# Attention of the second batch in five steps per slice, its rows in SBUF for the mixing, sums of two batches on VectorE, and one further place per tile afterwards

## The chip, the cores and the metric

One core of one Trainium2 chip runs the whole program in one launch. The metric is device time in microseconds (us). Before the change it is 1882.68 us, the median of three runs (1882.22 to 1883.0).

## What is computed

Three stages follow each other, on 8 batches of 576 tokens with 512 channels (8 heads of 64): attention with pooled keys and values, a mixing layer with two large matrix products, and a spectral layer with two more.

```python
k_p = k.reshape(B, H, Sp, pool, D).mean(axis=3)          # Sp = 72
v_p = v.reshape(B, H, Sp, pool, D).mean(axis=3)
scores = scale * np.matmul(q, k_p.transpose(0, 1, 3, 2))
attn = np.exp(scores - np.max(scores, axis=-1, keepdims=True))
attn = attn / (np.sum(attn, axis=-1, keepdims=True) + 1e-09)
x = np.matmul(attn, v_p)                                  # -> (B, S, 512)
u = x + (x.transpose(0, 2, 1) @ U @ V).transpose(0, 2, 1) # mixing, rank 32
x1 = u + np.maximum(u @ w_ch1, 0.0) @ w_ch2
u2 = x1 + np.real(np.fft.fft(np.fft.fft(x1, axis=1), axis=2))
out = u2 + np.maximum(norm(u2) @ w_ch1b, 0.0) @ w_ch2b
```

## The kernel before

Each float32 operand of a large product is split into a high and a low part (`split`, L109 and L110: ScalarE rounds the high part, the low part is a subtraction, L104), and three products of the parts are added.

**The large products of the first layer.** The tokens are cut into blocks of 256, and two blocks make a group. Group 0 to group 5 are worked off in a loop of 16 *slices* each (`for f in range(NF)`). A slice is `st1` (12 matmuls of 512 columns into bank h0, from the transposed tokens `utx` and the weights) and `st2` of the slice before (12 matmuls into four banks, from `hh` and `hl`). `utx` has three places for blocks, so a group's two blocks need `utx` filled before its first `st1`. After group 5 come the remaining tokens and the second layer, with another product scheme.

**What runs between them.** Generators called lanes are stepped at fixed points of a slice: lane "a" (attention) at three points, "w" (weights), "p" (`pair_prep`: load the next group's rows of `ud` in transposing pieces, `load_blocks` L801, transpose them on VectorE, L832, and split them into `utx`), "prep" (loads and pooling of keys and values), later "d" (spectral layer). In lane "a" one tile of 128 rows of a batch goes through: `kq` (8 matmuls into banks s0 and s1, maxima on VectorE, L548, eight exponentials on ScalarE, L551, each with its sum read out by `accum_out`), two steps later `exp_turn` (5 transposes, copies to `e`), one step later `av` (10 matmuls into s0, the rows `x` scaled by VectorE, L571, split into `xh` and `xl`, and stored to HBM, `xd`), and two steps later the next `kq`, with `hu_mm` of the tile before behind it (two matmuls `hu<-xh`, `hu<-xl`). After five tiles `mix_split` makes `hst` from `hu`, and `mix_one` computes u of each tile: load `x` back from `xd` (`mix_load`, L595, two buffers), one matmul `hst` by `vst` into bank s1, an add on VectorE (L107), a store to `ud` (L131).

Batch 0 goes through `tile_steps` ahead of all slices. Batch 1 goes through lane "a" inside group 0, and its mixing has steps of its own behind its attention. The mixing of batches 2 to 6 stands beside the next batch's attention. Group 1 consists of tokens 512 to 1023, so it needs the first four tiles of batch 1 mixed and stored.

**What sets the order.** Up to the end of group 0 a scheduler orders the instructions of every engine from the dependencies. From group 1 on TensorE, ScalarE and VectorE keep the order in which the code emits them. All loads and stores named here are issued by SyncE's one queue (SP), in order.

Of the kernel before, what the change touches and what calls it, by code (L numbers as in the profile page):

```python
# [8 lines left out]
F32 = mybir.dt.float32  # L9
# [39 lines left out]
def kernel(  # L49
# [80 lines left out]
    def store(o, i):  # L130
        later(lambda: nc.sync.dma_start(out=o, in_=i))  # L131
# [200 lines left out]
    class Attn:  # L332
# [113 lines left out]

        def xtile(self, b):
            return self.p.tile([128, DM], F32, tag="xr", name="x", bufs=2)

# [11 lines left out]
        def tile_steps(self, b, t, alt=0, before=None):  # L461
# [21 lines left out]
            for i in range(2):  # L483
                h = slice(4 * i, 4 * i + 4)
                v = sc[i][:n, 0:288].rearrange("p (h k) -> p h k", h=4)
                nc.vector.tensor_reduce(out=mx[:n, h], in_=v, op=ALU.max, axis=AX.X, negate=True)
                for k in range(4):
                    a = 4 * i + k
                    nc.scalar.activation(out=s[:n, a], in_=v[:, k], func=ACTF.Exp, bias=mx[:n, a:a + 1], accum_out=sm[:n, a:a + 1])
            yield  # L490
# [45 lines left out]
        def kq(self, b, t):  # L536
# [9 lines left out]
            for i in range(2):  # L546
                v = sc[i][:, 0:288].rearrange("p (h k) -> p h k", h=4)
                nc.vector.tensor_reduce(out=mx[:, 4 * i:4 * i + 4], in_=v, op=ALU.max, axis=AX.X, negate=True)  # L548
                for k in range(4):
                    a = 4 * i + k  # L550
                    nc.scalar.activation(out=s[:, a], in_=v[:, k], func=ACTF.Exp, bias=mx[:, a:a + 1], accum_out=sm[:, a:a + 1])  # L551
            self.cur = sm
# [12 lines left out]
        def av(self, b, t):  # L565
# [9 lines left out]
            split(xh, xl, xf)  # L575
            store(xd[b][t], xf[:TT[t][1]])
            self.done[t] = xh, xl
# [7 lines left out]
        def mix_mm(self, b, t, x):  # L585
            r0, n = TT[t]
            o = mbank()
            mm(o, self.vst[:, r0:r0 + 128], self.hst, True, True)
# [491 lines left out]
    def lane_a(at):  # L1080
        for b in range(1, B):
            while b not in ready:
                yield
# [7 lines left out]
            for t in range(5):  # L1091
# [3 lines left out]
                yield  # L1095
                yield
                at.exp_turn()
                yield
# [5 lines left out]
                yield  # L1104
                yield
            at.hu_mm(b, 4, *at.done.pop(4))
            at.mix_split(b)
            yield
            if b in (1, B - 1):
                at.mix_load(b, 0)  # L1110
# [114 lines left out]
    for gi, js in enumerate(groups):  # L1225
# [4 lines left out]
        for f in range(NF):  # L1230
# [31 lines left out]
            for i in range(3):  # L1262
                step("a")
                if i != 1:
                    step("d")
                if prev and i < 2:
# [216 lines left out]
```

## Time and profile before

| | us |
|---|---|
| median of 3 runs | 1882.68 |
| the profiled execution's own time | 1883.03 |
| its span in the trace | 1881.3 |
| TensorE busy in the span | 1811.7 (96%) |
| VectorE, ScalarE, GpSimd busy | 1017.3, 707.2, 194.7 |
| TensorE busy between 176 and 203 us | 9.46 of 27.0 |

Times in the trace count from the span's start; 1.7 us of the run lie outside the span. Group 0's first `st1` starts at 65.61 us, group 1's at 202.87 us. The program is one long sequence of matmuls with two stretches in which TensorE stands: up to 65 us, and from 176 to 203 us.

### The profile page before, as it was taken

To read this page: it belongs to the slowest core of one execution; us is meant where nothing else is said; L and a number is where in the kernel's file an instruction comes from. 1 tells how busy PE (TensorE), PEld (TensorE's weight loads), DVE (VectorE), ACT (ScalarE), POOL (GpSimd) and SP (SyncE) were. 2 spreads that over 40 slices of the span, in tenths; PEclk is the share of its full clock that TensorE was granted. 3 is DMA by queue.
4 is the path that set the end of the run, shared out by engine and by line. 5 is a ranking of instruction groups with operands and counts; after the bars stand their busy time and mean duration, and the time that the engine had idled before them with its cause. 6 is when DMAs were issued, how large, how long until landed. Compare 5 with 4: busy or idle time off the path is not lost.

```text
span 1881.3 us, 29486 instructions
## 1 busy us (share of the span) xinstructions
PE 1811.7 (96%) x10424; PEld 1584.6 (84%) x10424; DVE 1017.3 (54%) x2265; ACT 707.2 (38%) x2072; POOL 194.7 (10%) x341
## 2 busy tenths in 40 slices
PE   5798899999999999999999999999999999999999
PEld 4676688878788788898998889899999999999998
DVE  6763566757656534444555765555554444444322
ACT  7762354555454222233333433333323323232321
POOL 3430132222200000000000000000000000000000
PEclk8899799999999999999999999999999999999999
DMA  9753547877766722567767876777677675767674
GB/s 357 265 164 103 163 159 217 247 244 256 239 197 201 206 76 73 195 221 234 229 226 264 274 223 216 242 225 232 208 229 223 191 238 173 238 180 231 183 208 134
DMA packets 265779, 394.26 MB, mean 210 GB/s; under 512 B 61664, under 2 KB 92480, under 8 KB 265632
## 3 DMA queue, kind: packets, MB, share of 16 engines
q1 hardware_dynamic: 264704, 388.97, 66.5%
q0 software_dynamic: 928, 3.40, 0.6%
q8 instruction: 83, 1.36, 0.3%
q14 instruction: 64, 0.52, 0.1%
HBM read 312.73 MB, written 79.56 MB: 209 GB/s over the span
## 4 chain that ended last, share of the span: by engine, by line
PE 68%; DVE 2%; ACT 1%; DMA 1%; issue 0%; ACTq 0%; SPq 0%; DVEq 0%
PE h L114 31%; PE o L114 16%; PE m L114 8%; PE hu L114 7%; PE s L114 4%; PE s L927 1%; DMA wr<-wc 0%; DMA wd<-cv 0%; DMA x<-x 0%; DVE hl L1307 0%; DVE side L107 0%; ACT hh L1301 0%; PE s L557 0%; ACT s L551 0%; DVE hl L1015 0%
## 5 line engine op out<-in xcount | busy, mean ns | idle before, releaser
L114 PEld LDWEIGHTS h<-x,wr 128*128 128x128 f32 x4032 | 527.7, 191 | 26.1 <-DVE side L107 2.1
L114 PE MATMUL h<-x,wr 128*128 128x256 f32 x4032 | 547.6, 284 | 1.0 <-DVE side L107 1.0
L114 PE MATMUL o<-w,hh 128*128 128x512 f32 x1152 | 328.8, 396 | 3.2 <-ACT hh L1014 3.2
L114 PE MATMUL h<-utx,w 128*128 128x512 f32 (+1 forms) x1164 | 285.8, 395 | 1.4 <-ACT utx L110 1.2
L114 PEld LDWEIGHTS h<-utx,w 128*128 128x128 f32 x1164 | 218.8, 191 | 48.4 <-DVE hl L1015 1.4
L114 PEld LDWEIGHTS o<-w,hh 128*128 128x128 f32 x1152 | 202.7, 190 | 34.4 <-ACT hh L1014 4.1
L114 PE MATMUL o<-w,hl 128*128 128x512 f32 x576 | 192.3, 392 | 0.0
L107 DVE TENSOR_TENSOR side<-h,side 128x256 f32<-128x256 f32 x192 | 106.3, 553 | 150.2 <-PE h L114 149.6
L114 PE MATMUL m<-w,hh 128*128 128x512 f32 x576 | 164.4, 394 | 0.0
L1015 DVE SCALAR_TENSOR_TENSOR hl<-h,hh 128x512 fp32r<-128x512 f32 x96 | 66.3, 690 | 153.1 <-ACT hh L1014 152.9
L1301 ACT ACTIVATE hh<-side 128x256 fp32r<-128x256 f32 x192 | 99.9, 520 | 119.4 <-DVE side L107 115.4
L1301 ACT ACTIVATE hh<-h 128x256 fp32r<-128x256 f32 x96 | 36.8, 383 | 264.5 <-PE h L114 262.3
L1307 DVE SCALAR_TENSOR_TENSOR hl<-h,hh 128x256 fp32r<-128x256 f32 x96 | 40.7, 424 | 169.5 <-ACT hh L1301 169.5
L114 PEld LDWEIGHTS o<-w,hl 128*128 128x128 f32 x576 | 108.3, 188 | 24.2
L1307 DVE SCALAR_TENSOR_TENSOR hl<-side,hh 128x256 fp32r<-128x256 f32 x192 | 105.9, 551 | 29.4 <-ACT hh L1301 28.6
L114 PEld LDWEIGHTS m<-w,hh 128*128 128x128 f32 x576 | 102.2, 189 | 16.5
L1014 ACT ACTIVATE hh<-h 128x512 fp32r<-128x512 f32 x96 | 57.1, 594 | 148.6 <-PE h L114 148.5
L114 PE MATMUL hu<-w,hh 128*128 128x512 f32 x384 | 104.8, 394 | 0.0
L551 ACT ACTIVATE s<-s,mx 128x72 f32<-128x72 f32 x280 | 85.6, 329 | 44.8 <-DVE mx L548 44.4
L114 PE MATMUL m<-w,hl 128*128 128x512 f32 x288 | 97.3, 392 | 0.0
L104 POOL TENSOR_TENSOR wo<-wo 128x256 fp32r<-128x256 f32 x88 | 67.8, 789 | 267.9 <-ACT wo L110 154.5
L104 DVE TENSOR_TENSOR x<-ul,x 128x256 fp32r<-128x256 f32 x154 | 59.3, 421 | 47.6 <-ACT x L110 47.6
(250 smaller groups left out, 2421.7 us busy)
## 6 DMA issues: line engine op xcount, KB each, us to landing
wr<-wc SPq DMA_DIRECT2D x336, 512.0 KB
wc<-wo SPq DMA_DIRECT2D x88, 256.0 KB
x<-x SPq DMA_DIRECT2D x56, 256.0 KB
ur<-ud SPq DMA_DIRECT2D x36, 256.0 KB
x1d<-ur SPq DMA_DIRECT2D x36, 256.0 KB
ul<-u2d SPq DMA_DIRECT2D x36, 256.0 KB
ur<-u2d SPq DMA_DIRECT2D x36, 256.0 KB
out<-ur SPq DMA_DIRECT2D x36, 256.0 KB
```

The costliest lines, as they stand in the source:

```text
L104: eng.tensor_tensor(out=o, in0=a, in1=b, op=ALU.subtract)
L107: eng.tensor_tensor(out=o, in0=a, in1=b, op=ALU.add)
L114: nc.tensor.matmul(o, a, b, start=start, stop=stop, skip_group_check=True)
L551: nc.scalar.activation(out=s[:, a], in_=v[:, k], func=ACTF.Exp, bias=mx[:, a:a + 1], accum_out=sm[:, a:a + 1])
L927: nc.tensor.transpose(o[:, k * 128:k * 128 + 128], u[:, k * 128:k * 128 + 128], ident)
L1014: nc.scalar.activation(out=hh, in_=o, func=ACTF.Relu)
L1015: nc.vector.scalar_tensor_tensor(out=hl, in0=o, scalar=0.0, in1=hh.bitcast(F32), op0=ALU.max, op1=ALU.subtract)
L1301: nc.scalar.activation(out=hh[:, i], in_=c, func=ACTF.Relu)
L1307: nc.vector.scalar_tensor_tensor(out=hl[:, i], in0=c, scalar=0.0, in1=hh[:, i].bitcast(F32), op0=ALU.max, op1=ALU.subtract)
```

## The change

Five edits:

1. **Steps.** In group 0 lane "a" is stepped five times per slice and not three.
2. **Rows kept.** For batch 1 `xtile` hands out a tile of the pool `wo` (five buffers, 128 x 512 values, used otherwise by the weight lanes). `av` no longer stores it; it is put into `self.xm[t]`, and lane "a" mixes tile by tile from there, one step each, with no `mix_load`. Its `mix_mm` alternates between banks s1 and s0.
3. **Sums.** In batches 0 and 1 the exponentials have no `accum_out`; one `tensor_reduce` over 8 x 72 values per partition on VectorE makes a tile's sums (10 tiles in all).
4. **Places.** From batch 2 on there is one more step between `kq` and `exp_turn` and one less between `av` and the next `kq`.
5. **Start.** Batch 2 waits until slice 15 of group 0 has come.

```diff
         def xtile(self, b):
+            if b == 1:
+                return self.wo().rearrange("p h x -> p (h x)").bitcast(F32)
             return self.p.tile([128, DM], F32, tag="xr", name="x", bufs=2)
...
-                    nc.scalar.activation(out=s[:n, a], in_=v[:, k], func=ACTF.Exp, bias=mx[:n, a:a + 1], accum_out=sm[:n, a:a + 1])
+                    nc.scalar.activation(out=s[:n, a], in_=v[:, k], func=ACTF.Exp, bias=mx[:n, a:a + 1])
+            nc.vector.tensor_reduce(out=sm, in_=s, op=ALU.add, axis=AX.X)
...
-                    nc.scalar.activation(out=s[:, a], in_=v[:, k], func=ACTF.Exp, bias=mx[:, a:a + 1], accum_out=sm[:, a:a + 1])
+                    kw = {} if b == 1 else {"accum_out": sm[:, a:a + 1]}
+                    nc.scalar.activation(out=s[:, a], in_=v[:, k], func=ACTF.Exp, bias=mx[:, a:a + 1], **kw)
+            if b == 1:
+                nc.vector.tensor_reduce(out=sm, in_=s, op=ALU.add, axis=AX.X)
...
-            store(xd[b][t], xf[:TT[t][1]])
+            if b == 1:
+                self.xm[t] = xf
+            else:
+                store(xd[b][t], xf[:TT[t][1]])
...
-            o = mbank()
+            o = bank("s0") if b == 1 and t % 2 else mbank()
             mm(o, self.vst[:, r0:r0 + 128], self.hst, True, True)
...
-            while b not in ready:
+            while b not in ready or (b == 2 and state["slot"] < NF - 1):
                 yield
...
                 yield
                 yield
+                if b > 1:
+                    yield
                 at.exp_turn()
                 yield
                 at.av(b, t)
...
                 yield
-                yield
+                if b == 1:
+                    yield
             at.hu_mm(b, 4, *at.done.pop(4))
             at.mix_split(b)
             yield
-            if b in (1, B - 1):
+            if b == 1:
+                for t in range(5):
+                    at.mix_one(b, t)
+                    yield
+            if b == B - 1:
...
                 if i != 1:
+                    if gi == 0:
+                        step("a")
                     step("d")
```

**Place 1, between group 0 and group 1.** TensorE, from the first mixing matmul of batch 1 (`hst` by `vst`) to group 1's first `st1` (`h0<-utx`). The rows with `k`, `ident` and `v` are batch 2's first tile. Before:

```order
L114 MATMUL s1_1394<-hst_1358,vst_132 128x512
L114 MATMUL s1_1420<-hst_1358,vst_132 128x512
L114 MATMUL s1_1464<-hst_1358,vst_132 128x512
L114 MATMUL s1_1510<-hst_1358,vst_132 128x512
L114 MATMUL s1_1532<-hst_1358,vst_132 128x512
L114 MATMUL s1_1579<-k_126,q_1163 128x144 x2
L557 MATMUL s0_1651<-ident_69,s_128 128x128 x2
L558 MATMUL s1_1652<-ident_69,s_128 128x128
L114 MATMUL s0_1672<-v_127,e_1658 128x128
L114 MATMUL s0_1672<-v_127,e_1658 128x192 x3
L114 MATMUL s0_1672<-v_127,e_1658 128x64
L114 MATMUL h0_1703<-utx_122,w_420 128x512 x12
```

and now:

```order
L114 MATMUL s1_1262<-hst_1259,vst_132 128x512
L114 MATMUL s0_1283<-hst_1259,vst_132 128x512
L114 MATMUL s1_1286<-hst_1259,vst_132 128x512
L114 MATMUL s0_1295<-hst_1259,vst_132 128x512
L114 MATMUL s1_1304<-hst_1259,vst_132 128x512
L114 MATMUL s0_1611<-k_126,q_1111 128x144 x2
L114 MATMUL s1_1612<-k_126,q_1111 128x144 x2
L563 MATMUL s0_1652<-ident_69,s_128 128x128 x4
L564 MATMUL s1_1653<-ident_69,s_128 128x128
L114 MATMUL h0_1672<-utx_122,w_425 128x512 x12
L114 MATMUL s0_1689<-v_127,e_1659 128x128
```

The mixing alternates banks, all of batch 2's first `kq` stands behind it (half of it and two transposes stood ahead of it before), and batch 2's first `av` has moved behind the `st1`. In both programs the mixing stands behind the 16th `st1` of group 0.

At the same place SyncE's queue, from the first store of batch 1's mixed rows (`ud`) on; `x1_` are batch 1's rows in HBM, `ul<-ud` the transposing loads. Before:

```order
L131 DMA ud_116<-x_1367 128x512
L131 DMA ud_116<-x_1369 128x512
L595 DMA x_1409<-x1_2_83 128x512
L801 DMA ul_1456<-ud_116 32x16x32 x2
L595 DMA x_1448<-x1_3_84 128x512
L801 DMA ul_1456<-ud_116 32x16x32 x2
L131 DMA ud_116<-x_1409 128x512
L131 DMA ud_116<-x_1448 128x512
L801 DMA ul_1478<-ud_116 32x16x32 x4
L595 DMA x_1486<-x1_4_85 64x512
L801 DMA ul_1567<-ud_116 32x16x32 x3
L131 DMA ud_116<-x_1486 64x512
```

and now:

```order
L131 DMA ud_116<-wo_858 128x512
L131 DMA ud_116<-wo_1001 128x512
L131 DMA ud_116<-wo_1087 128x512
L131 DMA ud_116<-wo_1163 128x512
L810 DMA ul_1334<-ud_116 32x16x32
L131 DMA ud_116<-wo_1239 64x512
L810 DMA ul_1334<-ud_116 32x16x32 x3
L444 DMA q_1617<-qT 128x4x128
L810 DMA ul_1347<-ud_116 32x16x32 x4
L810 DMA ul_1387<-ud_116 32x16x32 x4
L810 DMA ul_1417<-ud_116 32x16x32 x4
```

The three loads of `x` are gone, the stores stand together, and the sixteen transposing loads follow with one store and one load of `q` between them.

**Place 2, group 0's first product.** TensorE, from the last transposes of batch 0's rows on. Before:

```order
L817 MATMUL h0_559<-ident_69,scr14_135 128x128 x4
L817 MATMUL s1_566<-ident_69,scr15_136 128x128 x4
L114 MATMUL s0_768<-k_126,q_362 128x144 x2
L114 MATMUL h0_573<-utx_122,w_420 128x256 x24
L114 MATMUL s1_769<-k_126,q_362 128x144 x2
L557 MATMUL s0_859<-ident_69,s_128 128x128 x2
L114 MATMUL o0_706<-w_423,hh_598 128x512 x2
```

and now:

```order
L826 MATMUL h0_564<-ident_69,scr14_135 128x128 x4
L826 MATMUL s1_571<-ident_69,scr15_136 128x128 x4
L114 MATMUL h0_578<-utx_122,w_425 128x256 x24
L114 MATMUL s0_773<-k_126,q_365 128x144 x2
L114 MATMUL s1_774<-k_126,q_365 128x144 x2
L114 MATMUL o0_711<-w_428,hh_603 128x512 x2
```

Batch 1's first `kq` (`s0<-k,q`) has moved from ahead of the first `st1` to behind it.

**Place 3, a tile of batch 2 in group 1.** TensorE, from `av` (the end of it) to the next tile's `hu`. Before:

```order
L114 MATMUL s0_2061<-v_127,e_2048 128x64
L114 MATMUL h1_1836<-w_528,hh_1965 128x512 x2
L114 MATMUL h1_1836<-w_528,hl_1966 128x512
L114 MATMUL m_1840<-w_528,hh_1965 128x512 x2
L114 MATMUL m_1840<-w_528,hl_1966 128x512
L114 MATMUL h0_2092<-utx_122,w_647 128x512 x12
L114 MATMUL s0_2109<-k_126,q_1852 128x144 x2
L114 MATMUL s1_2110<-k_126,q_1852 128x144 x2
L114 MATMUL hu_1740<-xh_2069,ust_130 128x512
L114 MATMUL hu_1740<-xl_2070,ust_130 128x512
```

and now:

```order
L114 MATMUL s0_1961<-v_127,e_1946 128x64
L114 MATMUL h1_1811<-w_493,hh_1863 128x512 x2
L114 MATMUL h1_1811<-w_493,hl_1864 128x512
L114 MATMUL m_1815<-w_493,hh_1863 128x512 x2
L114 MATMUL m_1815<-w_493,hl_1864 128x512
L114 MATMUL s0_1983<-k_126,q_1719 128x144 x2
L114 MATMUL s1_1984<-k_126,q_1719 128x144 x2
L114 MATMUL hu_1733<-xh_1969,ust_130 128x512
L114 MATMUL hu_1733<-xl_1970,ust_130 128x512
```

Six matmuls stand between `av` and the next `kq`, where 18 stood; twelve matmuls of `st1` have moved from there to between `kq` and `exp_turn`.

## Rows read from the trace of the kernel before

**Rows 1.** Page, first part: busy us, share of the span, instructions.

```profile
PE 1811.7 (96%) x10424; PEld 1584.6 (84%) x10424; DVE 1017.3 (54%) x2265; ACT 707.2 (38%) x2072; POOL 194.7 (10%) x341
```

**Rows 2.** Stretches: length, busy by engine (instructions), granted clock, DMA share, GB/s.

```profile
65.60:176.00 110.40, 105.87 (x511) 87.66 (x510) 62.98 (x103) 59.11 (x169) 31.64 (x28) 0.99 0.48 150
...
176.00:203.00 27.00, 9.46 (x25) 5.88 (x25) 10.64 (x19) 5.86 (x22) 0.00 (x0) 0.58 0.60 152
```

**Rows 3.** TensorE's timeline, 50 to 100 us: start, us, instructions, [idle before].

```profile
64.66 1.33 PE L114 MATMUL s<-k,q 128*128 128x144 f32 x4 [5.89 <-ACT k L423]
65.61 3.97 PE L114 MATMUL h<-utx,w 128*128 128x256 f32 x24
...
71.12 1.20 PE L114 MATMUL o<-w,hh 128*128 128x512 f32 x4 [0.83 <-ACT hh L1014]
```

**Rows 4.** VectorE's timeline, 40 to 105 us.

```profile
51.60 1.78 DVE L153 SCALAR_TENSOR_TENSOR cv<-wraw,cv 128x512 int32<-128x512 int32 x1
53.41 0.69 DVE L104 TENSOR_TENSOR hst<-hu,hst 32x512 fp32r<-32x512 f32 x1
...
62.95 0.73 DVE L413 TENSOR_REDUCE kp<-raw 128x72 f32<-128x576 f32 x1
...
64.81 0.67 DVE L104 TENSOR_TENSOR utx<-s,utx 128x512 fp32r<-128x512 f32 x1
```

**Rows 5.** ScalarE's timeline, 0 to 42 us: the first exponentials of batch 0.

```profile
15.81 0.19 ACT L489 ACTIVATION_READ_ACCUMULATOR s<-s,mx 128x1 f32 x1
15.90 0.31 ACT L489 ACTIVATE s<-s,mx 128x72 f32<-128x72 f32 x1
```

**Rows 6.** ScalarE's timeline, 40 to 105 us: batch 1's scaled keys.

```profile
63.71 0.89 ACT L423 ACTIVATE k<-kp 64x288 f32<-64x288 f32 x2 [0.63 <-DVE kp L413]
```

**Rows 7.** TensorE's timeline, 150 to 240 us.

```profile
175.57 0.40 PE L114 MATMUL hu<-xl,ust 128*128 128x512 f32 x1
...
177.97 0.51 PE L114 MATMUL s<-hst,vst 128*128 128x512 f32 x1 [0.77 <-DVE hst L104]
...
202.87 5.30 PE L114 MATMUL h<-utx,w 128*128 128x512 f32 x12 [1.17 <-ACT utx L110]
...
215.60 1.53 PE L114 MATMUL s<-v,e 128*128 128x128 f32 x10
216.94 0.71 PE L114 MATMUL o<-w,hh 128*128 128x512 f32 x2
```

**Rows 8.** VectorE's timeline, 160 to 212 us.

```profile
178.51 0.69 DVE L107 TENSOR_TENSOR x<-s,x 128x512 f32<-128x512 f32 x1 [0.60 <-PE s L114]
...
201.44 0.71 DVE L832 STREAM_TRANSPOSE ul<-ul 128x512 f32<-128x512 f32 x1 [1.66 <-DMA ul<-ud]
```

**Rows 9.** SyncE's queue, 140 to 212 us: issues (start, us).

```profile
179.23 1.60 SPq L131 DMA_DIRECT2D ud<-x  x2
...
181.62 1.34 SPq L801 DMA_DIRECT2D ul<-ud  x2
...
196.10 2.60 SPq L801 DMA_DIRECT2D ul<-ud  x4
```

**Rows 10.** Instruction groups between 176 and 203 us: the mixing's adds.

```profile
L107 DVE TENSOR_TENSOR x<-s,x 128x512 f32<-128x512 f32 (+1 forms) x5 | 3.4, 690 | 6.8 <-DMA x<-x 5.7 <-PE s L114 1.2
```

**Rows 11.** TensorE's waits between 400 and 500 us.

```profile
PE s L557 <- ACT s L551: 1.9, 5, 1.0
```

**Rows 12.** TensorE's timeline, 305 to 345 us: two times `av`.

```profile
308.97 1.53 PE L114 MATMUL s<-v,e 128*128 128x128 f32 x10
...
322.38 1.53 PE L114 MATMUL s<-v,e 128*128 128x128 f32 x10
```

**Rows 13.** VectorE's timeline, 305 to 345 us: the scaling behind these two.

```profile
310.54 0.69 DVE L571 TENSOR_TENSOR x<-s,sm 128x512 f32<-128x512 f32 x1 [0.81 <-PE s L114]
311.99 0.69 DVE L104 TENSOR_TENSOR xl<-x,xh 128x512 fp32r<-128x512 f32 x1 [0.76 <-ACT xh L110]
...
325.56 0.68 DVE L571 TENSOR_TENSOR x<-s,sm 128x512 f32<-128x512 f32 x1
```

## What the change will do to the time

> **What bounds the kernel now.** I read first the page's busy shares: TensorE is busy 96% of the span, the next engine 54% [rows 1]. So the end moves by what TensorE waits and by what it runs at the lower clock. Then the table of stretches: between 65.6 and 176 us, which is group 0, TensorE idles 110.4 - 105.87 = 4.5 us at its full clock (0.99). Between 176 and 203 us it is busy for 9.46 of 27 us, at a granted clock of 0.58, that is mostly at its lower level of 1.2 GHz [rows 2]. The third view is TensorE's timeline at both borders. At the first product it stood 5.89 us until batch 1's scaled keys `k` came from ScalarE, because a `kq` of batch 1 stands ahead of the first `st1` in its order [rows 3]. At the second border the last matmul of batch 1's attention (`hu<-xl`) starts at 175.57, the first mixing matmul at 177.97, and group 1's first `st1` only at 202.87 [rows 7]. What lies between is one chain: mixing, store to `ud`, transposing loads, transposes, split, `st1`. SyncE's queue and VectorE's timeline tell its pace [rows 8, 9], and the groups of this stretch say that VectorE's five adds waited 5.7 us for loads of `x` [rows 10].
>
> **Border between group 0 and 1 (the main term).** The five steps per slice alone do nothing here: in the new order batch 1's last `hu` and its mixing still stand behind the 16th `st1`, as before. What changes is the chain. Half a `kq` and four exponentials of batch 2 no longer stand ahead of `hst`, so I put the first mixing matmul 1.0 us earlier, at 177.0 on the old clock face. Its add starts 0.54 us later and takes 0.69 (177.97 to 178.51, [rows 7, 8]), so it ends at 178.2, and with two banks and no loads the other adds follow at VectorE's pace. The first store is issued at 178.2. In the trace the first transposing load went out 2.4 us behind the first store, with another load between them [rows 9]; I take 2.2 us and get 180.4. Now sixteen transposing loads stand nearly together. Four in a row take 2.60 us [rows 9], so sixteen 10.4 us; with one store and one load of `q` between them (0.4 us each, an estimate below the 0.65 of a transposing load) the last is issued at 180.4 + 11.2 - 0.65 = 191.0. The last load of the old chain was issued near 198.1 (196.10 and three of four) and its transpose began at 201.44, 3.3 us later [rows 8, 9]. So the new last transpose begins at 194.3, and `st1` follows as before by 1.43 us (201.44 to 202.87), at 195.7: 7.2 us earlier. Against it: batch 2's first `av` ran inside the hole and now stands behind the `st1`. Its ten matmuls take 1.34 us from start to start (215.60 to 216.94, [rows 7]). The term is -7.2 + 1.3 = **-5.9 us**. Its ends are -3 (the loads land later when they come in one row, or batch 2's exponentials, now ahead of all four splits in ScalarE's queue, hold them up) and -8 (a last landing one microsecond faster and no `q` in the way). The hole stays some 20 us long, so I give the clock no gain: the `st1` behind it takes 5.30 us at the lower level [rows 7], before and after.
>
> The Trainium skill's page "DMA: Bandwidth & Descriptors" (section "Anatomy of one DMA — SWDGE (gpsimd) path") gives one DMA about 2.0 us fixed plus its bytes over 436 GB/s; by that a store and a load of 256 KB in a row are 2.6 us each, and the two rounds that two buffers of `x` force would be an estimated 10.4 us. The row says that VectorE lost 5.7 us to those loads [rows 10]. With 10.4 in place of the 7.2 the total would be near 1871 us. The figure is for another queue's path, and the trace decides.
>
> **Group 0's first product.** Its operands come from batch 0's `hst`, at 53.41 on VectorE; the last split into `utx` starts at 64.81 [rows 4]. In the old order 18 VectorE instructions stand from `hst` up to that split, 11.40 us or 0.63 each; 17 stand there now, 10.8 us. Ahead of `hst` there are five new sums. The nearest row is a `tensor_reduce` over 576 values per partition, 0.73 us [rows 4]: +3.7 us on VectorE. Three weight instructions of 0.7 to 1.8 us (one at 51.60, [rows 4]) have moved behind `hst`, about -3. ScalarE is relieved of 40 read-outs at 0.09 us (15.81 to 15.90, [rows 5]), 3.6 us, and VectorE waited for ScalarE there at times. I take `hst` 1 us earlier, 52.4, and the last split starts at 63.2. The first `st1` no longer waits for `k`. But its `hh` stands behind `k` on ScalarE, and `k` waits for four more VectorE instructions behind the last split, 2.8 us: 63.2 + 0.7 + 2.8 = 66.7; `k` takes 0.9 [rows 6]; I allow 0.8 for `hh` (from the end of `st1` at 69.58 to `st2` it was 1.54 with half a `kq`, [rows 3]). So `st2` starts near 68.4 and not at 71.12 [rows 3], -2.7. Since the place of `hst` is the least certain thing here I take **-2.5 us**, with ends 0 (`hst` 2 us late under the sums) and -5 (2 us earlier still).
>
> **Inside group 0.** Five more sums on VectorE, 3.7 us in 110 us of which it is busy 62.98; 3.6 us off ScalarE, busy 59.11 [rows 2]. The 4.5 us that TensorE idles there are several short waits: **0**, between -2 and +2. The stores of five tiles fall away; TensorE's order holds nothing that waits for them.
>
> **From group 1 on.** The exponentials have three steps until `exp_turn` and not two. The waits for them (1.9 us in five between 400 and 500 us, [rows 11]) can go: about -2. In return six matmuls stand between `av` and the next `kq` where 18 stood: 1.33 us, by 5.30 for twelve at half the clock [rows 7]. `kq` writes the bank that the scaling reads. The `av` of 308.97 ends at 310.50; its scaling ends at 311.23, 0.73 us behind it, and `xl` at 312.68, 2.18 behind it [rows 12, 13]. `kq` now comes at 1.33 and, with its eight matmuls at some 1.0 us, `hu<-xl` near 2.5. It fits, with 0.3 to 0.6 us to spare. For the `av` of 322.38, which ends at 323.91, scaling ended at 326.24, 2.33 us behind the end, since VectorE was busy with other work [rows 12, 13]; there `kq` would wait 1 us. Two of 28 tiles were like this in the old order; I charge +2. Batch 2 starts a slice later and so does what follows; the transposes for group 2 stand closer to their loads, and I see no wait over 2 us there. **0 us**, between -3 and +6.
>
> **Sum.** -5.9 - 2.5 + 0 + 0 = -8.4 on the profiled execution's 1883.03 us (span 1881.3 and 1.7 around it): 1874.6. That execution is 0.35 above the median of 1882.68, so **1874.3 us**.
>
> **Rivals.**
> - *The later place bites (slower).* If VectorE's scaling ends 0.6 us or more too late behind most `av`s, `kq` waits each time. Two thirds of the 30 tiles of batches 2 to 7 have the short gap: 20 x 0.6 = 12 us give 1886, 20 x 1.0 give 1894. It decides from where scaling ends over 1.33 us behind `av`. The 0.73 of the one tile speaks against it, the 2.33 of the other for it [rows 12, 13].
> - *The start gives nothing.* The sums push `hst` back by 2 us: 1874.3 + 2.5 = 1876.8.
> - *The sixteen loads hold each other up.* In one row they land 3 us later: 1877.3. The DMA share of 0.60 in the old hole leaves room [rows 2].
> - *Both, or a few microseconds late after `av`:* 1879 to 1882.
> - *The change does more than I read.* The round of store and load costs 10 us, 1871; or, against the order of TensorE, batch 1's mixing leaves the hole altogether and most of its 17.5 idle microseconds go, 1862.
>
> **How the numbers follow.** Forecast (1871.5 to 1876.5) 0.50; start gives nothing 0.15; loads hold each other up 0.11; both or a little late after `av` 0.11; more than I read 0.08; the later place bites 0.05. A measurement of this kernel tells about 0.2%, 3.8 us, from no change, so faster is below 1878.9: 0.50 + 0.15 + 0.11 + 0.08 = 0.84. The fourth is no change, 0.11, the last slower, 0.05. The range is 1868.5 to 1880.5: the ends of the two main terms give 1869.7 (-8 and -5) and 1879.7 (-3 and 0), with about a microsecond for group 0 and what follows; it leaves out the slow rival, the 1862 and the tail of the fourth case.
>
> **What would show it.** The hole: group 1's `st1` starts 19 to 21 us behind the last `hu`, with no load of `x` in it, sixteen transposing loads in one row, and a granted clock still halved. The start: no `kq` ahead of the first `st1`, `st2` near 68. After 210 us the waits of L557 for the exponentials are gone and small ones for the scaling or `xl` have come. Wrong would be: a first product later than 65.6, a hole over 25 us, or more than 5 us of waits for the scaling after 210 us.

## The result: 1892.5 us, slower by 10

The changed kernel takes 1892.47 us, the median of four runs (1891.17 to 1893.72). The kernel before took 1882.45 beside it (1880.35 to 1883.0). The ratio is 1.0055, with a 95% interval of 1.0038 to 1.0073. The forecast was 1874.3, faster; the time lies outside its range. The profiled execution took 1891.17 us, with this page (busy time, share of the span and number of instructions of an engine):

```profile
span 1889.1 us, 29426 instructions
PE 1812.9 (96%) x10424; PEld 1588.1 (84%) x10424; DVE 1029.2 (54%) x2275; ACT 700.1 (37%) x1992; POOL 191.2 (10%) x341
```

TensorE has the same 10424 matmuls and nearly the same busy time (1811.7 before). The span grew by 7.9 us through what it waits for. Where, is read by setting the same matmul of both traces side by side:

| the same matmul | before, us | after, us | difference |
|---|---|---|---|
| first `st1` of group 0 | 65.61 | 61.41 | -4.2 |
| `st1` of slice 1 | 73.07 | 70.58 | -2.5 |
| `st1` of slice 15, the last of group 0 | 171.19 | 169.69 | -1.5 |
| first `st1` of group 1 | 202.87 | 194.97 | -7.9 |
| `st1` of slice 32 | 328.08 | 321.15 | -6.9 |
| `st1` of slice 48 | 454.09 | 449.80 | -4.3 |
| `st1` of slice 69 | 617.49 | 621.16 | +3.7 |
| second layer, matmul 1008 of `h<-x,wr` | 1062.15 | 1061.95 | -0.2 |
| the same, matmul 1176 | 1113.87 | 1121.25 | +7.4 |
| the same, matmul 3948 | 1850.76 | 1858.55 | +7.8 |

One trace tells such a place to 1 or 2 us: b_spec_later below, whose code up to there is that of the kernel before, starts the `st1` of slice 15 at 169.83. So the start and the border did what was forecast, and were 7.9 us ahead at 195 us. Behind that, 11.6 us were lost between 195 and 621 us, and 4.1 more up to the end. The last rows of the table hold work that only comes later, too: the spectral lane stands a slice later, which makes the second layer's start look early (-0.2) and the next stretch look long.

**The border**, as in [rows 2, 7 to 9]. TensorE idles 13.6 us in the hole and not 17.5, still at a granted clock of 0.57. Two stretches (length, then busy time and count of PE, PEld, DVE, ACT and POOL, granted clock, DMA share, GB/s):

```profile
61.40:169.69 108.29, 102.69 (x491) 86.20 (x492) 69.66 (x107) 57.35 (x129) 35.43 (x30) 0.97 0.43 135
175.00:195.00 20.00, 6.43 (x19) 3.70 (x19) 9.82 (x18) 5.82 (x22) 0.00 (x0) 0.57 0.67 162
```

The timelines of TensorE, SyncE's queue and VectorE there (start, time taken, engine, line, instruction, count, in brackets the idle time before it and what ended it):

```profile
175.35 0.73 PE L114 MATMUL s<-hst,vst 128*128 128x512 f32 x2 [1.41 <-DVE hst L104]
194.97 4.66 PE L114 MATMUL h<-utx,w 128*128 128x512 f32 x12 [11.31 <-ACT utx L110]
```

```profile
176.61 2.20 SPq L131 DMA_DIRECT2D ud<-wo  x4
178.91 0.66 SPq L810 DMA_DIRECT2D ul<-ud  x1
183.03 8.03 SPq L810 DMA_DIRECT2D ul<-ud  x12
```

```profile
193.54 0.71 DVE L841 STREAM_TRANSPOSE ul<-ul 128x512 f32<-128x512 f32 x1 [1.22 <-DMA ul<-ud]
```

Four stores stand in one row, the first transposing load follows the first store by 2.3 us (forecast 2.2), the sixteen loads have only a store and a load of `q` between them, and `st1` follows the last transpose by 1.43 us.

**Behind the border.** What TensorE waited for between 205 and 625 us (total, times, longest), first before, then after, the two largest of each:

```profile
PE s L114 <- ACT e L560: 2.9, 4, 1.6
PE s L557 <- ACT s L551: 2.4, 7, 1.0
```

```profile
PE s L114 <- DVE x L107: 12.1, 15, 1.3
PE s L114 <- DVE x L577: 2.1, 3, 1.6
```

All such waits in this stretch add up to 6.3 us before and 17.6 us after, which accounts for 11.3 of the 11.6 us lost.

The waits for the turn of the exponentials (L557, now L563) are gone. In their place stand 15 waits for `x` of L107, 12.1 us. L107 is an addition: that of the mixing (`mix_mm`), and not the scaling (L577). One place of the fifteen, batch 3's last-but-one tile, on TensorE, VectorE and ScalarE:

```profile
306.66 1.53 PE L114 MATMUL s<-v,e 128*128 128x128 f32 x10
307.99 0.48 PE L114 MATMUL s<-hst,vst 128*128 128x512 f32 x1
309.70 0.65 PE L114 MATMUL s<-k,q 128*128 128x144 f32 x4
311.02 0.76 PE L114 MATMUL s<-k,q 128*128 128x144 f32 x4 [0.67 <-DVE x L107]
```

```profile
308.22 0.69 DVE L577 TENSOR_TENSOR x<-s,sm 128x512 f32<-128x512 f32 x1
309.67 0.69 DVE L104 TENSOR_TENSOR xl<-x,xh 128x512 fp32r<-128x512 f32 x1 [0.76 <-ACT xh L110]
310.28 0.68 DVE L107 TENSOR_TENSOR x<-s,x 128x512 f32<-128x512 f32 x1
```

```profile
309.01 0.63 ACT L110 ACTIVATE xh<-x 128x512 fp32r<-128x512 f32 x1 [1.56 <-DVE x L577]
```

The mixing matmul follows `av` on TensorE and writes bank s1. Its add stands on VectorE behind the scaling and `xl`, and `xl` waits 0.76 us for ScalarE's `xh`. So the add ends at 310.96, 2.78 us behind the end of `av` (308.18). The next tile's `kq` came 1.51 us behind that end. Its first half writes s0, which the scaling left at 308.91, and starts at once. Its second half writes s1 and waits until the add has read it. Before, `kq` came 4.24 us behind such an `av` (that of 308.97 in [rows 12]) and met a free bank; that `kq`, and the add that had left the bank at 313.28:

```profile
314.74 1.14 PE L114 MATMUL s<-k,q 128*128 128x144 f32 x8
```

```profile
312.59 0.69 DVE L107 TENSOR_TENSOR x<-s,x 128x512 f32<-128x512 f32 x1
```

Ten of the fifteen waits are like the one shown (0.60 to 0.67 us). Behind the other five (0.92 to 1.29 us) VectorE was late with the scaling itself, which ended 1.05 to 3.23 us behind `av`. Batch 2, which has no mixing beside its attention, has no such wait in the changed kernel either.

**In the second layer** two waits between 1040 and 1130 us, after:

```profile
PE s L936 <- DVE ul L930: 3.0, 1, 3.0
PE s L114 <- DVE S L695: 1.9, 1, 1.9
```

The first of them (0.8 us before) is a transposition of normalised rows `ul`; behind it TensorE ran at a granted clock of 0.50 from 1096 to 1101 us. On VectorE four additions of the spectral lane (`F` and `R`, 1.34 us) stand right ahead of these rows' last steps, behind a weight split that waited for ScalarE; the first and the last row of that piece:

```profile
1093.38 0.69 DVE L104 TENSOR_TENSOR w<-w 128x512 fp32r<-128x512 f32 x1 [1.30 <-ACT w L110]
1093.99 0.42 DVE L107 TENSOR_TENSOR F<-F,S 128x256 f32<-128x256 f32 x1
...
1096.02 0.55 DVE L930 TENSOR_SCALAR ul<-ul,mv,rs 128x512 f32<-128x512 f32 x1
```

In the kernel before, those additions came at 1083 us. They are 1.3 of the 2.2 us by which this wait grew; the rest wasn't traced. The spectral lane begins when the attention lane has ended. With batch 2 held back its first matmul stands in slice 81 and not in 80, and the lane is out of step with the rows ever after.

### The profile page after: what moved, and what is told of

Same layout as the page of the kernel before. It is cut to its first block, busy times and chain, and to the rows that moved or that the text cites. A ratio compares the mean times of both kernels' runs of the same rounds, so it can differ in the third digit from the quotient of the medians.

```text
span 1889.1 us, 29426 instructions
## 1 busy us (share of the span) xinstructions
PE 1812.9 (96%) x10424; PEld 1588.1 (84%) x10424; DVE 1029.2 (54%) x2275; ACT 700.1 (37%) x1992; POOL 191.2 (10%) x341
## 4 chain that ended last, share of the span: by engine, by line
PE 83%; DVE 8%; DMA 3%; ACT 3%; issue 2%; SPq 1%; DVEq 0%; ACTq 0%
PE h L114 39%; PE o L114 19%; PE m L114 10%; PE hu L114 7%; PE s L114 7%; PE s L936 1%; DVE scr L154 1%; DMA ul<-ud 1%; DVE x L107 1%; DVE x L577 1%; ACT xh L110 1%; DVE scr L153 1%; PE s L563 1%; DMA raw<-vr 1%; DVE hl L1024 1%
## 5 line engine op out<-in xcount | busy, mean ns | idle before, releaser
L114 PE MATMUL h<-utx,w 128*128 128x512 f32 (+1 forms) x1164 | 285.3, 394 | 16.4 <-ACT utx L110 11.3
L107 DVE TENSOR_TENSOR side<-h,side 128x256 f32<-128x256 f32 x192 | 106.3, 554 | 153.5 <-PE h L114 153.0
```

The costliest lines, as they stand in the source:

```text
L107: eng.tensor_tensor(out=o, in0=a, in1=b, op=ALU.add)
L114: nc.tensor.matmul(o, a, b, start=start, stop=stop, skip_group_check=True)
```

## The experiments

Medians and ratios to the kernel before, run beside each (95% interval):

| kernel | median, us | ratio |
|---|---|---|
| changed kernel | 1892.47 | 1.0055 (1.0038 to 1.0073) |
| a_place_back | 1877.23 | 0.9972 (0.9961 to 0.9984) |
| a_mix_ahead | 1877.39 | 0.9972 (0.9961 to 0.9983) |
| a_s1_first | 1902.70 | 1.0098 (1.0082 to 1.0115) |
| b_place_only | 1887.65 | 1.0025 (1.0015 to 1.0036) |
| b_spec_later | 1884.26 | 1.0009 (1.0000 to 1.0018) |
| m_phase, measured twice | 1875.06, 1873.94 | 0.9962 (0.9949 to 0.9976), 0.9948 (0.9935 to 0.9962) |
| m_sums_back | 1877.50 | 0.9968 (0.9957 to 0.9980) |
| m_rows_stored | 1883.03 | 0.9998 (0.9987 to 1.0008) |
| m_no_hold | 1881.49 | 0.9994 (0.9984 to 1.0005) |
| p_phase | 1873.13 | 0.9952 (0.9937 to 0.9966) |
| p_min | 1888.36 | 1.0029 (1.0017 to 1.0041) |
| p_min_shift | 1873.91 | 0.9946 (0.9934 to 0.9959) |
| p_one_less | 1881.06 | 0.9988 (0.9980 to 0.9997) |
| m_two_less | 1887.17 | 1.0021 (1.0012 to 1.0030) |

### The mixing's bank

**a_place_back** takes edit 4 back:

```diff
                 yield
-                if b > 1:
-                    yield
                 at.exp_turn()
...
-                if b == 1:
-                    yield
+                yield
             at.hu_mm(b, 4, *at.done.pop(4))
```

> The changed kernel with the further place per tile taken back (two steps between kq and the turn of the exponentials, two behind av, for all batches); everything else of the change stays. Theory M (mixing's bank): with the further place, the next tile's kq comes one step after av, and its second half writes bank s1, which the add of the mixing matmul, issued right behind av, has not read yet; that wait is 12.6 us in 16 places of the changed kernel's trace. It then goes here, the waits for the exponentials (5.6 us in ten in the trace of the kernel before) come back: 1892.5 - 12.6 + 4 = 1884, and kq waits for the mixing add nowhere behind 210 us. Rival H (the hold): the loss from 210 to 610 us comes from batch 2 starting a slice later and all work behind it being pressed together; then 1890 to 1893 here.

1877.23 us: 15.2 us less than the changed kernel; 8.5 were expected. That is more than the 12.1 us of waits; the clock behind two of them, shown in the last section, is a part of the rest, which wasn't taken apart further. Between 205 and 625 us TensorE waits for no mixing add; what is left there is 7.2 us in 14 waits for `k`, `s` and `e`. Rival H falls: batch 2 is held back here as well.

**b_place_only** adds edit 4 alone to the kernel before; its diff is that of the two places with `yield` shown ahead of the prediction.

> The kernel before with the further place per tile alone. Theory M: batches 3 to 7 get the wait of the second half of kq for the mixing add, 12 us in some 16 places of 0.6 to 1.3 us, and lose some 4 us of waits for the exponentials: 1882.5 + 8 = 1890 to 1891. Batch 2, which has no mixing beside it, gets no wait. Rival H (the hold): 1879 to 1882, since only the waits for the exponentials go.

1887.65 us, slower by 5.0 where 8 were expected. The waits come, ten of them and not sixteen:

```profile
PE s L114 <- DVE x L107: 8.2, 10, 1.3
```

Two tiles of four per batch are hit, and three in the changed kernel: a tile has five steps and a slice three, so what stands between `av` and `kq` depends on where in a slice the batch began. Where an `st1` lies between them, there is no wait.

**a_mix_ahead** lets the mixing of the batch before go ahead of `av`, in the same step:

```diff
-                at.av(b, t)
                 if beside:
                     at.mix_one(b - 1, t)
-                    if t < 4:
-                        at.mix_load(b - 1, t + 1)
+                at.av(b, t)
+                if beside and t < 4:
+                    at.mix_load(b - 1, t + 1)
```

> The changed kernel with the mixing matmul of the batch before issued ahead of av and not behind it, in the same step; nothing else moves. Theory M: the mixing add then stands ahead of the scaling on VectorE, reads bank s1 while av still runs, and the bank is free long before kq: the 12.6 us go, 1880, with no wait of kq for the mixing add. Rival P (pace): kq one step behind av comes too early whatever stands there, and waits for the scaling in bank s0 or the split instead; then 1888 to 1892, with the waits under another name.

1877.39 us. TensorE and VectorE at the place shown above, which now comes at 305 us:

```profile
305.14 0.39 PE L114 MATMUL s<-hst,vst 128*128 128x512 f32 x1
305.37 1.53 PE L114 MATMUL s<-v,e 128*128 128x128 f32 x10
308.18 1.14 PE L114 MATMUL s<-k,q 128*128 128x144 f32 x8
```

```profile
306.58 0.68 DVE L107 TENSOR_TENSOR x<-s,x 128x512 f32<-128x512 f32 x1
307.18 0.68 DVE L577 TENSOR_TENSOR x<-s,sm 128x512 f32<-128x512 f32 x1
```

The add ends at 307.26, 0.92 us ahead of `kq`, which runs as one piece. `kq` stands where it stood, one step behind `av`. So rival P falls but for two tiles (339 and 483 us), where `kq` waits 1.71 and 1.85 us for the scaling, as three do in the changed kernel (2.1 us): the place is not too early, the add was too late.

**a_s1_first** takes nothing away. It moves the wait, by exchanging the score banks of the changed kernel's `kq`:

```diff
-            sc = bank("s0"), bank("s1")
+            sc = bank("s1"), bank("s0")
```

> The changed kernel with the two score banks of kq exchanged for batches 1 to 7: its first half writes s1, the second s0. Nothing is saved; a bound wait is moved. Theory M (mixing's bank): the mixing add that reads s1 ends some 2.8 us behind the end of av, and the half of kq that writes s1 now comes 0.6 us earlier; so the waits for that add grow from 0.6 or 0.7 to some 1.2 or 1.3 us each, now ahead of the first half, some 15 x 0.6 = 9 us in all: 1901 (1.010). Rival P (kq simply comes too early behind av, for whatever VectorE does last): the place of the wait is the same for both banks and the time stays at 1892 (1.0055).

1902.70 us, 10.2 more than the changed kernel, 1.7 from the expected time. The traces differ by 7.3 us (the profiled execution is the fastest of its four). The half that writes s1 now comes first, and waits 1.15 us where it waited 0.67:

```profile
PE s L114 <- DVE x L107: 21.3, 15, 3.6
```

```profile
312.93 1.25 PE L114 MATMUL s<-k,q 128*128 128x144 f32 x8 [1.15 <-DVE x L107]
```

With the bank the wait went to the other half. Thirteen of the fifteen are 1.09 to 1.47 us long, the other two 2.48 and 3.59. So the wait belongs to the bank that the add reads, and not to `kq`'s place as such.

### The phase of the spectral lane

**b_spec_later** is the kernel before with the spectral lane begun one slice later:

```diff
         if df or [name for name in lanes if name != "p"]:
             return
+        state["wait"] = state.get("wait", 0) + 1
+        if state["wait"] < 2:
+            return
```

> The kernel before with the spectral lane started one slice later (its start condition is let pass only at the second time it holds), as it is in the changed kernel; nothing else moves by hand. In the changed kernel 4.1 us were lost between 1060 and 1120 us against the kernel before, at a transposition that waited 3.05 us for VectorE and a spectral matmul that waited 1.86 us. Theory S (phase): this comes from the spectral lane being one slice out of step with the preparation of the third stage's rows; then 1886.5 here, with the same two waits near 1065 and 1092 us. Rival: it has another cause (what was loaded or stored differently); then 1882.5.

1884.26 us, an interval of 0 to 0.18% above the kernel before: less than expected, and hardly to be told from no change by the time alone. The trace has the two waits again, 1.86 us at 1063.78 and 3.05 at 1092.21:

```profile
PE s L927 <- DVE ul L921: 3.1, 1, 3.1
PE s L114 <- DVE S L686: 1.9, 1, 1.9
```

Set beside the kernel before, this run was 2.1 us ahead at slice 69 and 2.3 behind at the end; the whole swing lies behind slice 69.

**m_phase** is a_mix_ahead with two further spectral steps in slices 76 and 77, which put the lane back where it stood before:

```diff
                     step("d")
+                elif state["slot"] in (76, 77):
+                    step("d")
```

> The changed kernel with the mixing ahead of av (1877.4 us, 0.9972 of the kernel before) and two further steps of the spectral lane, in slices 76 and 77, so that from the Strassen products on it stands again at the places it had in the kernel before. Theory S (phase): the transposition that waited 3.04 us near 1083 us and the spectral matmul that waited 1.86 us near 1056 us go back to below 1 us, and the time falls by some 4 us, to 1873.5 (0.995). Rival: the phase is worth what the late start alone cost in the kernel before by the timed runs, 1.6 us; then 1875.8 (0.9963); or nothing, 1877.4.

1875.06 us and, measured again with 1875.1 expected, 1873.94: 2.3 and 3.5 us below a_mix_ahead, whose interval overlaps. The lane's first matmul stands in slice 80 again. Between 1040 and 1130 us the waits are those of the kernel before again:

```profile
PE s L936 <- DVE ul L930: 0.8, 1, 0.8
```

By the trace the correction is 2.6 us (spans of 1874.2 and 1871.6). So the phase is a real second cause; its size lies between 1.6 us (b_spec_later's time) and 4.4 (its trace, -2.1 to +2.3); the changed kernel's trace has 4.1.

### What the other parts are worth

Three kernels take one part each out of a_mix_ahead (1877.39).

**m_rows_stored** stores and loads batch 1's rows again.

```diff
         def xtile(self, b):
-            if b == 1:
-                return self.wo().rearrange("p h x -> p (h x)").bitcast(F32)
...
-            if b == 1:
-                self.xm[t] = xf
-            else:
-                store(xd[b][t], xf[:TT[t][1]])
+            store(xd[b][t], xf[:TT[t][1]])
...
-            o = bank("s0") if b == 1 and t % 2 else mbank()
+            o = mbank()
...
-            if b == 1:
-                for t in range(5):
-                    at.mix_one(b, t)
-                    yield
-            if b == B - 1:
+            if b in (1, B - 1):
```

> The same mended kernel (mixing ahead of av) with batch 1's rows stored and loaded again for the mixing, two buffers deep, on one bank, as in the kernel before; batch 2 still waits for the last slice. Theory: the rows kept in SBUF are the whole gain at the border between group 0 and 1 (6.4 us in the changed kernel's trace); then the hole between the last hu of batch 1 and the first st1 of group 1 grows from 20 to 26 or 27 us and the time is 1883.5 (1.0005). Rival: the order alone (batch 2 held back, no kq and exponentials of it in the chain) brought a part, and some 3 us stay: 1880.5 (0.999).

1883.03 us, as expected. Group 1's first `st1` starts at 201.46 and not at 194.97 (a_mix_ahead), 6.5 us later, 0.7 of them lost in group 0 already, and the waits for the five adds are back (170 to 205 us):

```profile
PE s L114 <- DVE x L107: 10.6, 5, 3.9
PE h L114 <- ACT utx L110: 6.8, 1, 6.8
```

**m_no_hold** lets batch 2 begin as soon as it is ready.

```diff
-            while b not in ready or (b == 2 and state["slot"] < NF - 1):
+            while b not in ready:
```

> The same mended kernel (mixing ahead of av) with batch 2 no longer held back until the last slice of group 0. Its first kq and exponentials then stand ahead of the mixing of batch 1, and the spectral lane starts earlier than in the kernel before. Theory: the border loses 1 to 2 us, the phase gives back some 2 to 4: 1874.5 to 1876.5 (0.996 to 0.997). Rival: without the hold batch 2's work ahead of the chain costs as much as the whole border gain, 6 us, and the phase gives nothing: 1883.

1881.49 us: the rival was near. The pooling of a later batch's values (`vp`) now stands ahead of `hst` on VectorE, and two tiles of batch 2 run inside the hole; the first `st1` starts at 200.49.

```profile
177.27 0.68 DVE L416 TENSOR_REDUCE vp<-raw 64x64 f32<-64x512 f32 x1 [1.11 <-DMA raw<-vr]
177.98 0.69 DVE L104 TENSOR_TENSOR hst<-hu,hst 32x512 fp32r<-32x512 f32 x1
```

So the border's gain needs both. From the `st1` of slice 15 to group 1's first it is 31.7 us in the kernel before, 25.0 in a_mix_ahead, 28.6 with kept rows and no hold, and 30.8 with the hold and no kept rows: 3.0 and 0.9 us alone, 6.7 together.

**m_sums_back** gives the sums of batches 0 and 1 back to ScalarE, in `kq` and in the same way in `tile_steps`.

```diff
-                    kw = {} if b == 1 else {"accum_out": sm[:, a:a + 1]}
+                    kw = {"accum_out": sm[:, a:a + 1]}
...
-            if b == 1:
-                nc.vector.tensor_reduce(out=sm, in_=s, op=ALU.add, axis=AX.X)
```

> The same mended kernel (mixing ahead of av) with the softmax sums of the first two batches given back to ScalarE, as in the kernel before. The first product started 4.2 us earlier in the changed kernel, 2.5 of which were left a slice later and 1.5 at the end of group 0. Theory A: this gain is the work of the sums (40 read-outs less on ScalarE ahead of the first mixing); then it falls away here, the first st1 starts near 65 us and the total is 1879 to 1880 (0.998 to 0.999). Theory B: it comes from batch 1's first kq standing no longer ahead of the first st1; then 1877 to 1878 and st1 stays near 62 us.

1877.50 us, as without. Theory A was right on the start and wrong on the time, and theory B the other way round: the first `st1` starts at 66.41 and not at 61.80, but that of slice 15 at 170.28 against 170.02. With the sums on VectorE the early start is given back inside group 0. (In seven other traces with the changed kernel's code up to there this `st1` starts between 170.0 and 171.6, so no gain is left that they could show.) VectorE is busy without a gap from 95 to 110 us, with the sums and without, and with them a product waits for `hh`; the changed kernel's row and its stretches:

```profile
102.02 1.58 PE L114 MATMUL o<-w,hh 128*128 128x512 f32 x4 [3.12 <-ACT hh L1023]
```

```profile
95.00:102.00 7.00, 3.90 (x19) 3.14 (x17) 7.00 (x10) 4.87 (x11) 5.13 (x4) 1.00 0.56 181
102.00:106.00 4.00, 3.98 (x12) 3.32 (x13) 4.00 (x7) 3.83 (x8) 3.24 (x3) 0.58 0.68 206
```

TensorE loses 3.1 us, and then runs at a granted clock of 0.58 for 4 us. With the sums on ScalarE it is busy for 6.15 us of the first stretch and not 3.90. That VectorE's load sets the end of group 0's middle is argued from these rows, not shown.

**p_phase** is a_place_back with the phase restored, and **p_min** takes out of it the five steps per slice and the sums (as in m_sums_back) as well.

```diff
                 if i != 1:
-                    if gi == 0:
-                        step("a")
                     step("d")
```

> The changed kernel with the further place per tile taken back and the two further spectral steps in slices 76 and 77. By the sum of the two corrections seen apart (1877.2 with the place taken back; 2.6 us by the trace for the phase) 1874.6 (0.9957); it compares with the mixing ahead of av and the phase (1875.1): if the further place was worth anything by itself, it stands 2 us or more above that, 1877.

> The same kernel as the one with the place taken back and the phase restored, and in addition without the five steps per slice in group 0 and with the sums of the first two batches back on ScalarE. What is left of the change is batch 1's rows kept in SBUF for the mixing and batch 2 held back. Theory: these two alone are the gain, and sums, five steps and place are worth nothing: 1874.5 to 1875.5 (0.996). Rival: the five steps bring the mixing of batch 1 into group 0's end or the sums give 2 us; then 1877 or more.

p_phase takes 1873.13 us, as m_phase: without the add in its way the further place shows no worth here. p_min takes 1888.36 (1882.64 to 1892.80 in twelve runs), 13 us more than expected. At group 1's first `st1` it was 8.7 us ahead of the kernel before, the best of all; by slice 69 it was 4.9 behind. From 205 to 625 us its two largest waits were:

```profile
PE s L114 <- ACT e L563: 6.1, 4, 3.2
PE s L560 <- ACT s L554: 3.9, 14, 1.1
```

Three kernels followed. **p_min_shift** is p_min with two further attention steps in slice 15 alone. **p_one_less** is p_phase with one step less there, **m_two_less** is m_phase with two less. Each does the same work as the kernel that it comes from; only the place in a slice at which batch 2 begins, and with it all batches behind it, is another.

```diff
                 if i != 1:
+                    if gi == 0 and f == NF - 1:
+                        step("a")
                     step("d")
```

In p_one_less and m_two_less:

```diff
-                    if gi == 0:
+                    if gi == 0 and (f < NF - 1 or i == 0):
...
-                    if gi == 0:
+                    if gi == 0 and f < NF - 1:
```

> The kernel with only batch 1's kept rows, batch 2 held back and the phase restored (1888.4), with two further attention steps in slice 15 alone, so that from group 1 on its attention stands in the slices where it stands with five steps per slice. Theory A (alignment): the loss of 12.7 us between 194 and 622 us was this shift of two steps and goes; 1874 (0.9955). Theory B (the parts themselves): the sums on VectorE or the five steps of the other fifteen slices are worth it; 1886 to 1889.

> The kernel with the place taken back and the phase restored (1873.1), with one attention step less in slice 15, so that batch 2 and all behind it stand one step later in their slices; no work is added or left out. Theory A (alignment): the time moves by several microseconds, to 1877 to 1886, with other waits of the turns and av for ScalarE between 200 and 620 us. Theory B: it stays at 1873 to 1875.

> The kernel with the mixing ahead of av, the further place and the phase restored (1874 to 1875), with two attention steps less in slice 15: the alignment at which the old place lost 13 us. Theory F: what the further place is worth is that the turn of the exponentials has three steps, so the alignment matters little with it; 1874 to 1877. Rival: the loss comes from the neighbours of that alignment, whatever the place; 1885 or more.

p_min_shift takes 1873.91: the 14 us are gone, and with them the reason to credit the sums, the further place or the steps of the other fifteen slices with anything. p_one_less takes 1881.06, and m_two_less 1887.17, so the further place doesn't protect from the shift: theory F falls. One of the places at which a shift costs time, p_min at 490 us, on ScalarE and TensorE:

```profile
487.01 0.66 ACT L110 ACTIVATE utx<-ul 128x512 fp32r<-128x512 f32 x1
489.30 0.43 ACT L149 ACTIVATE cv<-cv 128x256 f32<-128x256 f32 x1 [1.62 <-DVE wo L148]
489.63 0.58 ACT L1020 ACTIVATE hh<-h 128x512 fp32r<-128x512 f32 x1
490.11 0.59 ACT L563 ACTIVATE e<-s 128x512 f32<-128x512 f32 x1
```

```profile
490.84 3.01 PE L114 MATMUL s<-v,e 128*128 128x128 f32 x10 [3.24 <-ACT e L563]
```

```profile
491.00:496.00 5.00, 5.00 (x16) 4.52 (x17) 2.35 (x7) 0.63 (x1) 0.00 (x0) 0.50 0.26 96
500.00:505.00 5.00, 5.00 (x28) 4.11 (x27) 3.71 (x9) 3.72 (x19) 0.00 (x0) 1.00 0.95 284
```

Two splits of the next group's rows (the second of them is the first row), a step of a weight (`cv`) and an `hh` stand ahead of the copy of `e` in ScalarE's queue, and `cv` waits 1.62 us for VectorE. `av` waits 3.24 us for `e`; then TensorE runs at half the clock for some 5 us, so that the ten matmuls of `av` take 3.01 us and not 1.53. The prices of the other waits of these shifts weren't taken apart one by one.

## Why the prediction was wrong, point by point

- **Border: right, by two errors that cancel.** Forecast -5.9 (ends -3 and -8), measured -6.4 (from -1.5 to -7.9) at group 1's first `st1` and -6.2 at the next. With 1.5 us added for the shift of slice 15 the steps fell within a microsecond of the forecast, and `st1` starts 21.4 us behind the last `hu`, where 19 to 21 was said. But that `st1` was to come 7.2 us earlier and to lose 1.3 to the `av` behind it; it came 6.4 earlier, and 0.2 were lost up to the next. The clock, put at no gain, gave some: this `st1` took 4.66 us and not 5.30, at a granted clock of 0.68 between 195 and 200 us (0.55 between 203 and 208 before). The one estimate of the Trainium skill weighed there ("DMA: Bandwidth & Descriptors", section "Anatomy of one DMA — SWDGE (gpsimd) path": 10.4 us for two rounds of store and load) was too dear as a price of the border: without the kept rows it is 5.8 us longer (m_rows_stored against a_mix_ahead).
- **Group 0's first product: the number right, in part by luck, and it didn't last.** Forecast -2.5, and `st2` near 68.4; `st2` started at 68.64 and slice 1 was 2.5 us ahead. `hst` came at 49.17 on VectorE and not at the forecast 52.4, and from there to `st2` it was 19.5 us and not 16.0; the two errors cancel.
- **Inside group 0: in range.** Forecast 0 (-2 to +2), measured +1.0 (up to +2.5 in other traces with the same group 0). What was not seen is that this term and the one before belong together: m_sums_back starts 4.6 us later and ends group 0 within 0.3 us.
- **From group 1 on: wrong, and this decided.** Forecast 0, between -3 and +6; measured +11.6 up to slice 69. The step that failed is the sentence "`kq` writes the bank that the scaling reads". `kq` writes two banks. The prediction followed s0 (the scaling) and `xl` up to `hu`, found "0.3 to 0.6 us to spare", and left out s1, which the mixing matmul right behind `av` takes and whose add is the third of the chain behind `av` on VectorE. Both numbers were in the rows: 2.18 for the end of `xl` [rows 13] plus an add of 0.6 to 0.7 gives 2.8, against `kq` at 1.33 and its second half about 0.5 later. By that sum some 0.9 us a tile were due; the fifteen waits took 0.8 on average. The sign of being wrong that the prediction named, over 5 us of waits for the scaling, would have missed this: those waits were 2.1 us.
- **Spectral lane: not priced.** "Batch 2 starts a slice later and so does what follows" was written, but only the transposes for group 2 were looked at. That a lane which starts a slice later stays out of step in the second layer cost 1.6 to 4.4 us.
- **The rival that came true** is "the later place bites", with a chance of 0.05. Its size was right (20 x 0.6 = 12 us, against 15 waits and 12.1 us), its range of 1886 to 1894 holds the time. That it does is in part luck: the measured time lies 18.2 us above the forecast, of which these waits are 12.1, and the spectral lane, which the rival doesn't have, is a part of the rest. Its condition was wrong, too: it was to need a scaling that ends over 1.33 us behind `av`. The scaling ended 0.73 behind ten of the fifteen, as [rows 13] had it, and the bank of the add decided. With the right bank in its condition the rows would have spoken for it.
- **Steps: right at the border, incomplete behind it.** "The five steps per slice alone do nothing" holds for the border. But in slice 15 they set the place of every later batch, and p_min against p_min_shift shows that this is worth 14 us, more than any term of the sum. The changed kernel had the good place, and the prediction didn't know it.

## What to carry to other kernels

When an instruction moves closer to its predecessor, list every buffer that it writes, with the last reader of each and that reader's place in its own queue: the first buffer can be free while the second isn't. Lanes of five and of three steps that run beside each other have a phase, and an edit at one place can shift all that follows; measure such an edit at more than one phase before a part is credited. A lane that starts later keeps its offset long after its cause, so follow it to the end of the program. The gain here, 1873 to 1875 us or 0.5% below the kernel before, came with kept rows, the held batch, the restored spectral phase and a good place in slice 15; p_min_shift has these and no more. Without the good place the same parts took 1888.

## What the runs showed that was not expected

- A wait costs its length and at times the clock behind it, and its length alone didn't tell which. After the 3.24 us of p_min the granted clock was 0.50 between 491 and 496 us, and after the 3.12 us at 102 in the changed kernel 0.58 for 4 us; after p_min's 2.36 us at 337 it was 0.82 from 338 to 343, and after p_phase's 2.24 us at 540 it was 1.00 from 541 to 546. The six waits of 0.6 to 1.6 us of the changed kernel between 400 and 500 us left it at 1.00, but two of 0.36 and 1.29 us at 530 and 532 were followed by 0.59 for 4 us:

```profile
531.87 0.76 PE L114 MATMUL s<-k,q 128*128 128x144 f32 x4 [1.29 <-DVE x L107]
```

```profile
532.00:536.00 4.00, 4.00 (x13) 3.27 (x14) 2.58 (x8) 3.29 (x18) 0.00 (x0) 0.59 0.39 119
```

  The Trainium skill's page "TensorE: Matmul & The Clock Gate" (section "A second HAM failure mode: psum-queue depth-cycling") tells of a kernel whose short idles between groups of matmuls made the clock go up and down; in the changed kernel short waits did so at 530 us and not between 400 and 500.
- 4.6 us at the start of the first product were worth 0.3 us at the end of its group, which is less than two traces of the same code differ there.
